# First weights, first blocks and first state of a recurrent loop brought into the stage before it: a two-branch kernel on one core

## The chip, the cores and the metric

One Trainium2 chip, one of its cores. The metric is device time in microseconds from start to end of one execution. Engines are named as in the profile: PE (TensorE matmul), PEld (its weight load), DVE (VectorE), ACT (ScalarE), POOL (GpSimd), SP (SyncE, which issues most DMAs; its queue is SPq). POOL issues DMAs too (POOLq). L339 is line 339 of the kernel before.

## The reference, cut to what matters

The output is two independent branches side by side. Branch A is a transformer layer with a memory of 8 rows that runs over 64 segments of 32 rows; each segment needs the memory that the one before it left. Branch B is a long convolution: a kernel K is summed from exponentials and applied to u by FFT.

```python
def A(x, mem0, Wq, Wk, Wv, Wo):            # x 2048x1024, 32 heads of 128
    mem = mem0                              # 8 x 1024
    for s in range(64):
        h = concat([mem, x[32*s:32*s+32]])
        q, k, v = h @ Wq, h @ Wk, h @ Wv    # each weight 1024 x 4096
        p = softmax(where(mask, q k^T * scale, -1e9))
        o = (p v) @ Wo                      # 4096 x 1024
        mem, outs[s] = o[:8], o[8:]

def B(u, A, B, C, log_dt, Dskip):           # u 2048 x 1024, state 128
    K = einsum(C, exp(dt*A*l), dt*B).real   # 1024 x 2048
    y = irfft(rfft(pad(u)) * rfft(pad(K)))[:2048] + u*Dskip
```

Everything is bfloat16 at the borders. The four weights of A are 33.6 MB together, in units of 128x2048 (512 KB); 64 units make up one segment.

## The kernel before

The program has three stages, one after the other, whose order of instructions on each engine is the order in which they are written (a manual schedule; the framework adds the semaphore waits).

**Tables** (up to about 490 us). `part_b` builds the Fourier matrices `MF` (ACT sines), transposes x, projects the rows of A that don't depend on the memory (`Ahead.projections`), transforms u into `Ud` in DRAM (`side`), and makes the tables of K over 16 blocks in an order written out by hand (`ORDER`). K goes to DRAM as `Kd`. In round f = 15 its first half (512 of 1024 columns) is read back as `KT` (L938 on SP), and POOL negates half of that into `KN` (`negate`, L974, at the word "u0" of `ORDER`).

**Transform** (about 488 to 746 us). 16 rounds b (L1238 on). Round b issues: the spectrum matmuls of b+1 (`spectrum`, L989, 64 matmuls reading `MF`, `KT` and `KN`), the copies `odd` on ACT, `pointwise` of b on DVE (ten 128x1024 operations, L1162 to L1173, reading `uq`, which SP loads two rounds ahead, L965), and from b = 4 on two inverse blocks (`inverse`, L1216, 64 matmuls reading the inverse matrices `MI` and their negated copies `mn`, then ACT `yb`, two DVE operations and a store by POOL, L1226). Eight more inverse blocks follow the last round; their inputs `Bt` are complete only when `pointwise` of round 15 is. Round b reads only column block kc = b mod 4 of `MF`, but `MF` is laid out by row block first. In round 0 POOL reads the second half of K (31 DMAs, L938) and SP loads three weight units; `negate` of the second half is on ACT in round 6 (L976), ahead of that round's inverse blocks.

**Weights that stay.** Of the 64 units, 45 stay in SBUF over all segments, 2 (`KEPT`: k,0,7 and o,15) stay in PSUM and are copied out piece by piece on DVE (`words`, `fetch`, L278), and 17 are streamed from DRAM in every segment through five slots `wst` (L256). 34 of the 45 are loaded by the generator `residents` during the transform: 3 in round 0, 4 in round 6, 8 in round 14, the rest between the last eight inverse blocks. They go into tiles that are dead by then: `kst`, `MF`, `xTl`, `wsl`, and a pool over the transform's work tiles. The other 11 are loaded where the first segment first uses them (`unit`).

**Loop** (`part_a`, about 746 us to the end). Before it, POOL makes the constants (identity, masks), PE transposes `mem0` into the state `hT`, SP loads the two KEPT units, and DVE puts them in PSUM. Each segment: k, q, v of both halves (L339), scores, softmax, output projection (L438), new state. The loop's weights come in the order of use; SP waits at each streamed unit until the slot's last reader on PE is done.

The KEPT units are loaded like this (L280 to L282), into the slots that the first streamed units also take:

```python
    for i, key in enumerate(KEPT):
        t_ = wst.tile([128, 2048], BF16, name="wst", tag="w%d" % i)
        nc.sync.dma_start(out=t_[:].rearrange("e (h d) -> e h d", h=2) if key[0] == "o" else t_[:], in_=src(key))
```

Of the kernel before, what the change touches and what calls it, by code (L numbers as in the profile page):

```python
# [29 lines left out]
SLOTS = 5  # L30
# [147 lines left out]

RESIDENT = [(m, t, kc) for t in range(2) for m in "kq" for kc in range(8)] + [("v", t, kc) for t in range(2) for kc in range(8)] + [("o", u) for u in range(16)]
RESIDENT = [key for key in RESIDENT if key not in streamed_keys() and key not in KEPT]  # L180


class Keys(list):
    pass


EARLY = (3, 13)


def load_resident(tc, pool, src, key, W_res, eng=None, t_=None):  # L190
    if t_ is None:
        t_ = pool.tile([128, 2048], BF16, name="W_%s" % "_".join(str(i) for i in key))
    (eng or tc.nc.sync).dma_start(out=t_[:].rearrange("e (h d) -> e h d", h=2) if key[0] == "o" else t_[:], in_=src(key))
    W_res[key] = t_


def part_a(ctx, tc, x, mem0, src, WD, HE, seg_len, out_a, ahead, W_res, rest):
    nc = tc.nc
    S, Dm = x.shape
    M = mem0.shape[0]  # L200
    SL = seg_len
    E = 128
    KC = Dm // 128
    NS = S // SL
    assert SL == 32 and M == 8 and Dm == 1024 and HE == 4096
    XM = 24
    XL = SL - XM
    NK = SL + M
    scale = float(E ** -0.5)

    const = ctx.enter_context(tc.tile_pool(name="a_const", bufs=1))
    XTd, PKd, OLd = ahead.XTd, ahead.PKd, ahead.OLd

    ctx.enter_context(tc.manual_schedule())
    ctx_w = rest.ctx
    wst = ctx_w.enter_context(tc.tile_pool(name="a_wst", bufs=1, side="right"))
    wres = ctx_w.enter_context(tc.tile_pool(name="a_wres", bufs=1, side="right"))
# [19 lines left out]
    nc.gpsimd.affine_select(out=BDL[:], in_=BDL[:], compare_op=ALU.is_ge, fill=0.0, base=7, pattern=[[8, 4], [32, 4]], channel_multiplier=-1)  # L237

    loads = [0]
# [4 lines left out]
    def unit(key):  # L244
        if key in rest:

            rest.remove(key)
            load_resident(tc, wres, src, key, W_res)
        if key in W_res:
            return W_res[key]  # L250
        if key in kept:
            return ahead_of.pop(key)
        between.pop(key, lambda: None)()
        t_ = wst.tile([128, 2048], BF16, name="wst", tag="w%d" % (loads[0] % SLOTS))
        loads[0] += 1
        nc.sync.dma_start(out=t_[:], in_=WD[key][:])  # L256
        return t_

    hT = const.tile([128, KC, SL], BF16, name="hT")
    with tc.tile_pool(name="a_m0", bufs=1) as pm0, tc.tile_pool(name="a_pm0", bufs=1, space=PSUM) as ppm:  # L260
        m0 = pm0.tile([M, Dm], BF16, name="m0")
        nc.scalar.dma_start(out=m0[:], in_=mem0)
        pm = ppm.tile([128, KC, M], BF16, name="pm")
        for kc in range(KC):
            nc.tensor.transpose(out=pm[:, kc, :], in_=m0[:, kc * 128:(kc + 1) * 128], identity=ident[0:M, 0:M])
        nc.vector.tensor_copy(out=hT[:, :, XM:SL], in_=pm[:])
# [13 lines left out]
    for i, key in enumerate(KEPT):  # L280
        t_ = wst.tile([128, 2048], BF16, name="wst", tag="w%d" % i)
        nc.sync.dma_start(out=t_[:].rearrange("e (h d) -> e h d", h=2) if key[0] == "o" else t_[:], in_=src(key))  # L282
        kept[key] = [ps_k.tile([128, 512], F32, name="keep", tag="keep%d" % (2 * i + n)) for n in range(2)]
        for n in range(2):
            words(kept[key][n][:], t_[:, 1024 * n:1024 * n + 1024])
# [31 lines left out]
    put_xt(load_xt(0))  # L317
# [9 lines left out]

    fetch(("k", 0, 7))
    for s in range(NS):
# [267 lines left out]
def part_b(ctx, tc, u, A_re, A_im, B_re, B_im, C_re, C_im, log_dt, Dskip, out_b, ahead, copies, residents):  # L597
# [22 lines left out]
    MF = ahead.pool.tile([128, 16, 2, 512], BF16, name="MF", tag="MF")  # L620
# [10 lines left out]
    with tc.tile_pool(name="b_par", bufs=1) as par, tc.tile_pool(name="b_parh", bufs=2) as parh, tc.tile_pool(name="b_mg", bufs=2) as mg, \  # L631
# [50 lines left out]

        def matrices():

            tms, kMs = {}, {}
            for c in range(0, 20, 2):
                if 4 <= c:
                    tm = tms.pop(c - 4)
                    v.tensor_scalar(out=tm[:].bitcast(I32), in0=tm[:].bitcast(I32), scalar1=0x7FFFFFFF, scalar2=None, op0=ALU.bitwise_and)
                    sc.activation(out=MF[:, c - 4:c - 2, 0, :], in_=tm[:], func=ACT.Sin, scale=-TWO_PI, bias=hp[:])  # L690
                if 2 <= c < 18:
                    tm = tms[c - 2]
                    v.scalar_tensor_tensor(out=tm[:], in0=kMs.pop(c - 2)[:], scalar=MAGIC, in1=tm[:], op0=ALU.subtract, op1=ALU.subtract)
                    sc.activation(out=MF[:, c - 2:c, 1, :], in_=tm[:], func=ACT.Sin, scale=-TWO_PI)
# [108 lines left out]

    kxp = ctx1.enter_context(tc.tile_pool(name="b_kx", bufs=2))
    tmp = ctx1.enter_context(tc.tile_pool(name="b_tmp", bufs=2))
# [18 lines left out]
    def matrices_back():  # L824
        for c in range(16):
            mt = take([128, 2, 4, 128], BF16, "mt")
            for kc in range(4):
                for cs in range(2):
                    pe.transpose(out=mt[:, cs, kc, :], in_=MF[:, c, cs, 128 * kc:128 * kc + 128], identity=ident[:])
# [7 lines left out]
    def side():  # L837

        uvs = [load_uq(0), load_uq(1)]
        for dq in range(4):  # L840
# [3 lines left out]
            for kc in range(4):  # L844
                got = {}
                for r in (0, 2, 1, 3):
                    ps = take([128, 2, DQ], F32, "ups")
                    for cs in range(2):
                        for mc in range(4):
                            pe.matmul(ps[:, cs, :], lhsT=MF[:, 4 * r + mc, cs, 128 * kc:128 * kc + 128], rhs=uv[:, 4 * r + mc],  # L850
# [79 lines left out]
    def load_k(dh, qs, KT):  # L930
        dsl = slice(DH * dh, DH * dh + DH)
# [39 lines left out]
    def negate(KT, eng=None):  # L971
# [3 lines left out]
        else:  # L975
            sc.activation(out=KN[:], in_=KT[:, 8:16, :], func=ACT.Copy, scale=-1.0)  # L976
        KNs.append(KN)

    def spectrum(b, s_):
        dq, kc = b // 4, b % 4  # L980
        KT, KN = ks[dq // 2], KNs[dq // 2]
        d = slice(DQ * (dq % 2), DQ * (dq % 2) + DQ)
        for half in range(2):
# [396 lines left out]
```

## Time and profile before

| what | value |
|---|---|
| time, median of 3 runs | 2421.98 us (2419.69 to 2426.86) |
| the profiled execution, its own time | 2430.37 us |
| its span | 2428.7 us |
| PE, DVE, ACT, POOL busy | 83%, 61%, 40%, 14% of the span |
| moved by DMA | 759.08 MB, mean 313 GB/s |
| last matmul of the transform | 741.2 us |
| first matmul of the loop | 754.9 us |
| end of segment 0 (first `ob`, L527, start) | 795.38 us |
| last `ob`, segment 63 | 2368.5 us, so 24.97 us for a segment |

How to read it: a row of a timeline gives start and duration in us, engine, line, operation, output and input, and in brackets how long the engine sat idle before it and what released it. A table of windows gives for each stretch its length, the busy time of each engine with the number of instructions, the granted TensorE clock, the busy share of the DMA engines, and GB/s. A table of waits gives for "who <- whom" the total, the number and the longest wait in us.

### The profile page before, as it was taken

What the parts mean: (1) busy time and instruction counts of PE and PEld (TensorE: products, weight loads), DVE (VectorE), ACT (ScalarE), POOL (GpSimd) and SP (SyncE); (2) the same over time, 40 slices, a digit from 0 to 9 for tenths busy, and PEclk for the clock granted to TensorE, in tenths of its full rate; (3) what the DMA queues carried; (4) which work ended last, traced back from release to release, by engine and by line L of the source; (5) the groups of instructions that cost most, each with busy time, mean ns of one, the idle gap of its engine ahead of it and who ended that gap; (6) DMA issues with size and microseconds to landing.
All of it is one profiled execution on the core that took longest, in us unless ns stands there. A gap on an engine that the chain in (4) does not pass through costs nothing.

```text
span 2428.7 us, 78387 instructions
## 1 busy us (share of the span) xinstructions
PE 2009.3 (83%) x33798; PEld 1184.6 (49%) x33798; DVE 1480.1 (61%) x3159; ACT 976.1 (40%) x1598; POOL 345.6 (14%) x578
## 2 busy tenths in 40 slices
PE   1699999669996888888888888888888888888879
PEld 1366665558883444444444444444444444444444
DVE  9599999989972445455554545454545545454540
ACT  6699999603332233232333333332323233332321
POOL 2235445541121000000000000000000000000020
PEclk6799999879997899999999999999999999999999
DMA  6686974583368999999999999999999999999992
GB/s 160 183 250 195 255 213 146 163 254 138 116 251 313 374 360 365 382 367 384 370 380 379 386 387 383 383 374 376 370 369 374 376 384 365 383 367 380 386 385 75
DMA packets 379376, 759.08 MB, mean 313 GB/s; under 512 B 121144, under 2 KB 213272, under 8 KB 376980
## 3 DMA queue, kind: packets, MB, share of 16 engines
q1 hardware_dynamic: 365236, 710.86, 81.3%
q0 software_dynamic: 13776, 43.19, 5.3%
q8 instruction: 264, 4.33, 0.7%
q14 instruction: 84, 0.69, 0.1%
q10 hardware_dynamic: 16, 0.02, 0.0%
HBM read 699.16 MB, written 67.88 MB: 316 GB/s over the span
## 4 chain that ended last, share of the span: by engine, by line
DMA 34%; PE 26%; DVE 9%; issue 6%; ACT 3%; SPq 1%; POOL 1%; ACTq 0%; DVEq 0%; POOLq 0%
DMA wst<-WD_k 15%; PE acc L339 13%; DMA wst<-WD_o 12%; PE pp L438 3%; DMA wst<-WD_v 2%; PE pe L561 2%; PE tr L350 2%; DMA out_dram<-uu 2%; DMA wst<-WD_q 2%; DVE piece L278 2%; ACT ev L345 1%; PE hps L989 1%; DMA W_o<-in_A_Wo_dram 1%; PE yp L1216 1%; DVE ob L527 1%
## 5 line engine op out<-in xcount | busy, mean ns | idle before, releaser
L339 PEld LDWEIGHTS <-hT 128*32 128x32 bf16 x12352 | 328.4, 97 | 472.0 <-issue 251.4
L339 PE MATMUL acc<-wst,hT 128*32 128x512 bf16 x3072 | 313.7, 392 | 166.5 <-DMA wst<-WD_k 74.5
L345 ACT CAST ev<-acc 128x512 bf16<-128x512 f32 x384 | 224.7, 585 | 411.9 <-PE acc L339 406.0
L339 PE MATMUL acc<-W,hT 128*32 128x512 bf16 x4608 | 366.2, 388 | 0.0
L438 PEld LDWEIGHTS <-oT 128*32 128x32 bf16 x8192 | 204.8, 97 | 120.5 <-issue 95.3
L278 DVE TENSOR_SCALAR piece<-keep 128x256 int32<-128x256 int32 (+1 forms) x640 | 191.6, 363 | 58.0 <-PE pp L438 31.3
L438 PE MATMUL pp<-W_o,oT 128*32 128x256 bf16 x5120 | 212.5, 276 | 7.3 <-DMA W_o<-in_A_Wo_dram 7.2
L377 DVE TENSOR_REDUCE mx<-sc 128x8 f32<-128x320 f32 x128 | 62.4, 487 | 247.3 <-PE sc L370 247.2
L339 PE MATMUL acc<-W_v,hT 128*32 128x512 bf16 x3072 | 210.9, 379 | 0.0
L351 DVE COPY KT<-tr 128x512 bf16<-128x512 bf16 x64 | 27.2, 425 | 262.6 <-PE tr L350 262.6
L438 PE MATMUL pp<-wst,oT 128*32 128x256 bf16 x2560 | 129.3, 279 | 41.8 <-DMA wst<-WD_o 32.9
L358 POOL COPY KT<-pk 128x128 bf16<-128x128 bf16 x128 | 37.6, 294 | 806.8 <-PE sc L370 448.7
L351 ACT COPY QT<-tr 128x512 bf16<-128x512 bf16 x128 | 74.9, 586 | 192.1 <-PE tr L350 191.2
L425 ACT CAST oT<-pv 128x512 bf16<-128x512 f32 x128 | 74.9, 585 | 168.7 <-PE pv L411 166.4
L312 POOL COPY hT<-xt 128x192 bf16<-128x192 bf16 x64 | 22.2, 347 | 736.7 <-DMA xt<-XTd 536.2
L989 PEld LDWEIGHTS <-MF 128*128 128x128 bf16 x1024 | 104.4, 102 | 44.3 <-issue 24.3
L158 PE MATMUL pro<-xTl,wsl 128*128 128x512 bf16 x512 | 120.1, 386 | 5.2 <-ACT xTl L102 5.2
L1216 PE MATMUL yp<-Bt,MI 128*128 128x256 bf16 x768 | 114.9, 276 | 3.6 <-DVE Bt L1173 3.6
L379 ACT ACTIVATE sc<-sc 128x320 f32<-128x320 f32 x128 | 54.0, 422 | 153.6 <-DVE sc L378 149.6
L989 PE MATMUL hps<-KT,MF 128*128 128x256 bf16 x720 | 95.7, 286 | 20.6 <-DVE x L1163 17.5
L350 PEld LDWEIGHTS <-ev 128*128 128x128 bf16 x1024 | 58.4, 98 | 98.2 <-issue 67.9
L350 PE MATMUL tr<-a_ident,ev 128*128 128x128 bf16 x1024 | 102.5, 223 | 1.0 <-ACT KT L351 1.0
(302 smaller groups left out, 3704.6 us busy)
## 6 DMA issues: line engine op xcount, KB each, us to landing
wst<-WD_o SPq DMA_DIRECT2D x320, 512.0 KB
wst<-WD_k SPq DMA_DIRECT2D x256, 512.0 KB
wst<-WD_q SPq DMA_DIRECT2D x256, 512.0 KB
wst<-WD_v SPq DMA_DIRECT2D x256, 512.0 KB
Ud<-ux POOLq DMA_DIRECT2D x16, 1024.0 KB, 5.6
uq<-Ud SPq DMA_DIRECT2D x32, 512.0 KB
pk<-PKd SPq DMA_DIRECT2D x64, 192.0 KB
wsl<-in_A_Wk_dram SPq DMA_DIRECT2D x16, 512.0 KB
```

The costliest lines, as they stand in the source:

```text
L158: nc.tensor.matmul(a[:], lhsT=w[:, kc, 128 * j:128 * j + 128], rhs=xTl[:, kc, :, :].rearrange("p s k -> p (s k)"), start=(kc == 0), stop=( ...
L278: nc.vector.tensor_scalar(out=out.bitcast(I32), in0=in_.bitcast(I32), scalar1=0, scalar2=None, op0=ALU.bitwise_or)
L339: nc.tensor.matmul(a[32 * g:32 * g + 32, o_:o_ + rhs.shape[1]], lhsT=hT[:, kc, :], rhs=rhs, start=(kc == 0), stop=(kc == KC - 1), tile_pos ...
L345: nc.scalar.copy(out=q[:], in_=a[:])
L350: nc.tensor.transpose(out=p[:, i, hl, :, :].rearrange("p a b -> p (a b)"), in_=q[:, 128 * hl:128 * hl + 128], identity=ident[:])
L351: eng(out=dst, in_=p[:, i, :, :, :])
L377: nc.vector.tensor_reduce(out=mx[:], in_=sc, axis=AX.X, op=ALU.max)
L379: nc.scalar.activation(out=sc, in_=sc, func=ACT.Exp, scale=scale)
L425: nc.scalar.copy(out=o[:], in_=p[:].rearrange("p a (g q) -> p a g q", g=4))
L438: nc.tensor.matmul(po[32 * qt:32 * qt + 32, :], lhsT=oT[:, h % 4, (h % 16) // 4, :], rhs=columns(w, 1024 * hh + 256 * qt, 256)[0][1], star ...
L989: pe.matmul(s_[r][half][:, cs, :], lhsT=MF[:, 4 * rr + mc, cs, 128 * kc:128 * kc + 128], rhs=rhs, start=(i == 0 and mc == 0), stop=(i == 1 ...
L1216: pe.matmul(yp[:, b, :], lhsT=m_[:, b, cs, kc, :], rhs=Bt[:, kc, j, half, c_, :], start=(n == 0), stop=(n == 15), skip_group_check=True)
```

## The change

- `MF` is laid out by column block first, so that a finished column block is 32 KB a partition in one piece.
- `KT` of the second half of K is two tiles of 256 columns instead of one of 512 (62 DMAs by POOL instead of 31, the same bytes). These, the `MI` matrices (eight tiles of 4 KB a partition instead of one) and the three first weight units move to one pool on the right side of SBUF. `mn` and the tiles of the inverse blocks get places of their own, and `odd` has one buffer instead of two.
- The weight loads are spread otherwise: one in each of rounds 1 to 3, four in round 6, two in 11 and 12, four in 13 and 14, then 10, 5 and one at a time in the last eight inverse blocks. They go over `kst`, the dead column blocks of `MF`, the two `KT` tiles, `xTl`, `wsl`, four new tiles, and dead `MI` tiles.
- The five slots `wst` are opened before the transform ends, and the first five units that the loop takes through them are loaded there. The unit o,15 is loaded in the loop, ahead of v,0,0 of segment 0.
- The loop's constants are made in round 4, `mem0` and the first x are loaded there, and the state is made in round 13 (8 transposes on PE, a copy on DVE, a copy on POOL).
- After round 15, three quarters (kc 0 to 2) of the matmuls of the first three of the last eight inverse blocks are issued before the blocks themselves.
- `negate` of the first half stands at the word "m'" of `ORDER` in round 15 instead of "u0"; that of the second half stands behind round 6's inverse blocks instead of before them, in two operations.

```diff
-EARLY = (3, 13)
+EARLY = (3, 4)
+LATE = 5
...
-    MF = ahead.pool.tile([128, 16, 2, 512], BF16, name="MF", tag="MF")
+    MF = ahead.pool.tile([128, 4, 16, 2, 128], BF16, name="MF", tag="MF")
...
-            if f == 15 and word == "u0":
+            if f == 15 and word == "m'":
                 negate(ks[0], gp)
...
+    pool = ahead.ctx.enter_context(tc.tile_pool(name="a_wre1", bufs=1, side="right"))
+    KT2 = [pool.tile([128, 16, DQ], BF16, name="KT", tag="KT%d" % i) for i in range(2)]
+    MI = [pool.tile([128, 2, 2, 4, 128], BF16, name="MI", tag="MI%d" % i) for i in range(8)]
...
+    def inverse_begin(dq, c, yp):
+        ready.append(negated(c)) if len(ready) * 2 <= c else None
+        early[dq, c] = yp
+        products_back(yp, dq, c, *ready[c // 2], range(3))
...
         if b == 0:
-            ks.append(load_k(1, (gp,), ktp.tile([128, 16, DH], BF16, name="KT", tag="KT")))
-            for _ in range(EARLY[0]):
-                next(resident)
+            ks += [load_k(DQ * i, DQ, (gp,), KT2[i - 2]) for i in (2, 3)]
...
-        if b == 6:
-            negate(ks[1])
-            for _ in range(4):
-                next(resident)
-        if b == 14:
-            for _ in range(8):
-                next(resident)
...
+        for _ in range({1: 1, 2: 1, 3: 1, 6: 4, 11: 2, 12: 2, 13: 4, 14: 4}.get(b, 0)):
+            next(resident)
+        if b == 4:
+            state = first_state(iv.tile([8, D], BF16, name="m0", bufs=1), iv.tile([128, 8, 24], BF16, name="xt0", bufs=1))
+            next(state)
+        if b == 13:
+            state.send(ps_y.tile([128, 8, 128], BF16, name="yp", tag="yp")[:, :, 0:8])
         if b >= 4:
             inverses(2)
+        if b == 6:
+            negate(ks[1:])
+    begun = [ps_h.tile([128, 2, 2, DQ], F32, name="hps", tag="h") for _ in range(2)]
+    for n_ in range(3):
+        inverse_begin(3, 2 * n_, begun[n_ // 2][:, n_ % 2])
     ctx2.close()
-    for _ in range(8):
+    for n_ in range(8):
         inverses(1)
-        for _ in range(3):
+        for _ in range((10, 5)[n_] if n_ < 2 else 1):
             next(resident, None)
-    for _ in resident:
-        pass
...
+        ahead.wst = ctx_w.enter_context(tc.tile_pool(name="a_wst", bufs=1, side="right"))
...
+        for i, key in enumerate((("k", 0, 7), ("k", 0, 0), ("k", 0, 5), ("q", 0, 1), ("q", 0, 5))):
+            first[key] = t_ = ahead.wst.tile([128, 2048], BF16, name="wst", tag="w%d" % i)
+            tc.nc.sync.dma_start(out=t_[:], in_=WD[key][:] if key in WD else src(key))
+            yield
...
+    def first_state(m0, xt):
+        nc = tc.nc
+        hT = constants(tc, const, ahead)
+        nc.sync.dma_start(out=xt[:].rearrange("p k r -> p (k r)"), in_=ahead.XTd[0])
+        nc.sync.dma_start(out=m0[:], in_=A_mem0[0])
+        pm = yield
+        for kc in range(8):
+            nc.tensor.transpose(out=pm[:, kc, :], in_=m0[:, kc * 128:(kc + 1) * 128], identity=ahead.consts[0][0:8, 0:8])
+        nc.vector.tensor_copy(out=hT[:, :, ahead.XM:], in_=pm)
+        nc.gpsimd.tensor_copy(out=hT[:, :, 0:ahead.XM], in_=xt[:])
+        yield
...
-    for i, key in enumerate(KEPT):
+    def load_kept(key):
...
+    load_kept(("k", 0, 7))
     fetch(("k", 0, 7))
+    between["v", 0, 0] = lambda: load_kept(("o", 15))
```

## The prediction

> **What bounds the kernel now.** I read the windows by stage first, then the timelines of SP and DVE at the two places where the stages change hands, then the waits.
>
> ```profile
> 600.00:640.00 40.00, 40.00 (x369) 35.84 (x367) 37.80 (x41) 11.49 (x24) 8.67 (x12) 1.00 0.32 107
> 680.00:720.00 40.00, 36.38 (x319) 31.81 (x317) 34.85 (x40) 14.14 (x26) 7.96 (x11) 0.96 0.75 268
> 720.00:760.00 40.00, 25.74 (x239) 20.64 (x238) 9.07 (x23) 11.38 (x20) 12.93 (x35) 0.80 0.74 272
> 760.00:800.00 40.00, 27.42 (x422) 12.50 (x425) 13.04 (x36) 8.49 (x16) 0.64 (x2) 0.71 1.03 395
> 1000.00:1500.00 500.00, 423.83 (x8608) 223.33 (x8609) 261.33 (x726) 155.68 (x302) 19.00 (x61) 0.99 1.00 380
> ```
>
> After the stretch come PE, PEld, DVE, ACT, POOL, then clock, DMA share, GB/s. The transform (600 to 640) keeps PE busy all the time with DVE at 94% and DMA at a third; the loop (from 760) keeps DMA at 1.00 with PE at 85%. So transform time is PE time, loop time is bytes, and a byte moved from the loop into the transform costs nothing there. Between the two neither is full:
>
> ```profile
> 496.27 9.59 SPq L124 DMA_DIRECT2D PKd<-PVd  x8
> 505.90 1.48 SPq L1141 DMA_DIRECT2D Dsk<-in_B_Dskip_dram  x1
> 508.19 1.42 SPq L193 DMA_DIRECT2D W_k<-in_A_Wk_dram  x3
> 509.70 1.58 SPq L965 DMA_DIRECT2D uq<-Ud  x2
> ...
> 714.78 12.00 SPq L193 DMA_DIRECT2D W_v<-in_A_Wv_dram  x11
> 746.27 0.33 SPq L282 DMA_DIRECT2D wst<-in_A_Wk_dram  x1
> ```
>
> ```profile
> 735.00:742.00 7.00, 6.18 (x57) 5.28 (x54) 1.53 (x5) 2.14 (x5) 3.42 (x16) 1.00 0.55 205
> 742.00:749.00 7.00, 0.34 (x8) 0.27 (x8) 0.52 (x2) 0.00 (x0) 2.38 (x10) 0.66 0.29 78
> 749.00:756.00 7.00, 1.08 (x12) 0.53 (x16) 3.89 (x9) 0.00 (x0) 0.34 (x1) 0.50 0.69 240
> ```
>
> SP issues no load from 726.8 to 746.3: the next tile lies over the inverse blocks' tiles and waits for the last store (four waits of SP on `out_dram<-uu`, 19.2 us). PE ends the transform at 741.2 and starts the loop at 754.9. Segment 0 then ends at 795.38 (`ob`), 54.2 us after the last matmul of the transform. Three stalls stand inside the transform:
>
> ```profile
> 522.28 1.23 DVE L1167 TENSOR_TENSOR y<-uq,x 128x1024 f32<-128x1024 f32 x1 [7.62 <-DMA uq<-Ud]
> ```
>
> ```profile
> PE yp L1216 <- DVE Bt L1173: 3.6, 1, 3.6
> PE yp L1216 <- ACT mn L1188: 2.9, 1, 2.9
> ```
>
> **The change, part by part**, as what it takes from the end of segment 0. From there on the same 17 units, stores and instructions follow in the same order with the same waits, 24.97 us a segment, and the same final projection, so the gain passes through unchanged.
>
> *Three weight loads out of round 0.* DVE is ready for `uq` of round 2 at 514.66 (513.45 + 1.21), and it lands at 522.2. From 500 to 536 the DMA share is 1.0. On SP's queue ahead of `uq` stand eight PKd copies, Dsk and three weight units; the units (1.57 MB) go to rounds 1 to 3, behind `uq`. At the 357 GB/s of 512 to 522 they took 4.4 us, and SP issues `uq` up to 2.3 us earlier (509.70 against the end of Dsk, 507.38). I put the landing at 516.3, so 1.6 us of the stall stay and **6.0 us** go. Ends: 0 (the queue is full anyway, and K's second half now comes in 512-byte rows) and 7.6. The chain of waits goes from DVE here into PE at 534, so PE gets what DVE gets.
>
> *K in 62 pieces instead of 31.* POOL issued 31 in 498.5 to 520.4, 0.71 us each; 62 end at about 545, at the 0.55 us of those without a wait at 536. Behind them on POOL stand the five `uu` loads of the first inverse blocks, then the constants. The first `uu` is used at 557.1 (551 after the gain), and one takes 2.7 us to land: cover of 3 us at the slow pace. Cost 0; without the cover, 1 to 4 us. K itself is first used in round 7, at 585.
>
> *`negate` of the first half.* The Trainium skill, page "SBUF — State Buffer", section "Who interferes with whom", says that VectorE in a two-port mode and GpSimd contend for one pair of ports, and the second to issue blocks until the first is done. The row:
>
> ```profile
> 460.40 10.57 POOL L974 TENSOR_SCALAR KN<-KT 128x4096 bf16<-128x4096 bf16 x1 [1.27 <-DMA PVd<-vst]
> 462.51 9.44 DVE L1050 TENSOR_SCALAR nr<-nr 128x1856 int32<-128x1856 int32 x1
> ```
>
> The same operation took 1.6 us a round before (441.79), so the block costs 7.8 us. By the rule alone, an earlier place in the order would free them. But the bracket says that a DMA released it, not POOL: the last of the 31 KT loads was issued by SP up to 458.4, two microseconds before 460.4. Those don't move. The only POOL instruction passed is one store of `MId` (0.56 us), not needed until round 3. I take 0; the ends are 0 and 7.8 (the latter would need K earlier).
>
> *`negate` of the second half behind round 6's inverse blocks.* ACT ran it for 3.64 us at 579.96, ahead of `mn`, and PE waited 2.9. Now it starts when the second block's `yb` are out (about one us after PE goes on to the spectrum), and its first piece, 1.8 us, is needed 4.1 us into that spectrum (36 matmuls that read only KT). **2.9 us**; ends 0 and 2.9.
>
> *State and constants.* The constants took 4 us on an idle POOL (739.9 to 743.9); in round 4 they run beside `pointwise`, where DVE has 0.8 us a round to spare and can be a few us late without holding PE. 0; at worst 3. The 8 transposes in round 13 take one of two PSUM buffers, and by the waits in the built program the round's second block then waits for the copy (0.66 us) of the first: **-0.9 us**.
>
> *Three inverse blocks begun.* PE idled 3.62 us for `Bt`, and then eight blocks took 28.5 us (712.71 to 741.2) at a clock of 0.79 at first, where 3.49 us a block make 27.9. Now 3 x 3/4 x 3.49 = 7.9 us of them fill the gap. Gained 3.6 + 0.6, lost 0.9 since the second block shares a PSUM tile with the first and waits for its `yb`: **3.3 us**; ends 0 and 4.2.
>
> PE so ends the transform 6.0 + 2.9 - 0.9 + 3.3 = 11.3 us earlier, at 729.9.
>
> *Units placed over dead tiles.* The 27 units that were issued from 693.8 on become 12 in rounds 11 to 14, where two thirds of DMA are free, and 20 after (five of them the loop's first). Fourteen of these wait until `pointwise` of round 15 is done (about 705); with 2 MB of `uu` they are 9.3 MB, 24 us at 385 GB/s: in by 730, as PE ends. On SP they stand behind the `uq` of rounds 13 to 15, which are needed 11 us after issue while two units take 2.8. In MI's eight loads of 512 KB for four of 1 MB a rule speaks against the change: the skill's "DMA: Bandwidth & Descriptors", section "Measured (HBM→SBUF, 128 partitions, SWDGE, issued from GpSimd)", wants 1 MB or more for 75% of peak; by its fixed 2.0 us (section "Anatomy of one DMA"), one after another, four more loads would add 8 us. The row of the loop, 512 KB a load at 380 GB/s with up to eight in flight, makes it nothing. I take the row.
>
> *The handover.* Before: 54.2 us from PE's last transform matmul to `ob`. After: k,0,7 and k,0,0 lie in their slots and the state is ready. SP's first blocked load (k,1,0) waits for DVE to empty slot 0: `yb` 0.7 and the last two `uu` operations 0.5 after PE's end, then two copies of 0.63, 2.5 us together. From there 12 streamed units, o,15 and 11 resident ones, 24 x 0.524 MB and 0.25 MB of pk and xt, at 380 GB/s: 33.8 us; the last one lands and is used 2.4 us later (in the loop the last pp takes 1 us and `ob` follows 0.3 after). Sum 38.7, **15.5 us** less. PE needs about 24 us for a segment, so it stays under that. Ends: 9 (the 1.6 us a unit that segment 0 needs before, 48 us for 30, on 24 units, and 7 us of start) and 27 (no idle DMA at all from 705 on).
>
> Sum 11.3 + 15.5 = 26.8. Against its own execution: 2430.37 - 26.8 = 2403.6; against the median, which is 8.4 us lower, 2421.98 - 26.8 = **2395.2 us**.
>
> **Rivals.** *The front stays full* (20%): 512-byte rows and MI use the room that the units leave, `uq` still lands at 521 to 522, or `uu` comes late by what is gained. For it: DMA at 1.0 until 536. Against: bytes ahead of `uq` on its own queue fall by a third. 2395 + 6 = 2401. *The handover packs better* (13%): the loads fill DMA so that segment 0 ends with its transfers from 694 on, 44 units at 1.38 us and 4 us of `uu`, near 760. For it: 399 GB/s in 699 to 738. Against: eight in flight, and five slots that only the loop frees. Gain 35 to 40, so 2384. *Longer segments* (4%): slots and resident tiles lie elsewhere, the segment is DMA bound at 1.00, and every wait added there counts 63 times. It decides from 26.8/63 = 0.43 us a segment; at 0.6 the time is 2395 + 38 = 2433. For it: only that no slack exists. Against: the waits listed for the loop's loads are those of before. *It doesn't do what it says* (5%): the loads in rounds 11 to 14, waiting on SP for the last spectrum matmul of their column block, hold the `uq` behind them, and each round stretches. Four rounds at 2 us, gain 19, 2403. Against: that spectrum ends before the `pointwise` which frees the `uq` tile.
>
> **How the numbers follow.** 58% for 2395, with its own range 2388 to 2402 from the ends of `uq` and the handover. Of the rivals, the first and the last lie at 2401 to 2404, the second at 2384: with those two sides in, 2381 to 2406 holds 8 in 10. 0.3% is 7 us, about what a measurement of this kernel can tell from no change. Slower by more: 4%, the third rival. Within: 3%, where several gains fail together. Faster: 93%.
>
> **What would show it.** Right: no SP gap between the last resident load and a slot load; DVE's stall before L1167 of round 2 under 3 us; no `yp` wait on `mn` in round 6; PE going from the last `yp` to `acc` within 2 us at a clock of 1.00; segment 0 over 35 to 42 us after that; 24.9 to 25.0 us a segment. Wrong: a DVE stall on `uu` at round 4, `uq` waits in rounds 12 to 15, KN starting well before 460, or segments longer than 25.3 us.

## The result, and the profile after

The changed kernel takes 2396.86 us (median of 4 runs, 2393.12 to 2401.22) where the kernel before takes 2423.1 us (median of 4): a ratio of 0.9892, with a 95% interval of 0.9865 to 0.9919. That is 26.2 us less; the forecast was 26.8. The profiled execution takes 2401.22 us against 2430.37 us, 29.2 us less.

Windows of the changed kernel, with the columns as before (length, PE, PEld, DVE, ACT, POOL, clock, DMA share, GB/s):

```profile
600.00:640.00 40.00, 40.00 (x369) 35.85 (x367) 38.57 (x43) 13.81 (x26) 8.67 (x12) 1.00 0.37 117
...
680.00:720.00 40.00, 38.76 (x354) 34.35 (x353) 29.90 (x38) 16.86 (x29) 9.41 (x13) 1.00 0.81 287
720.00:735.00 15.00, 13.90 (x152) 10.48 (x150) 5.47 (x14) 3.85 (x10) 6.07 (x9) 1.00 1.00 368
735.00:742.00 7.00, 5.54 (x109) 2.37 (x105) 1.42 (x3) 3.25 (x5) 0.30 (x1) 1.00 1.03 406
742.00:749.00 7.00, 5.71 (x111) 2.51 (x112) 6.40 (x17) 3.18 (x7) 0.00 (x0) 1.00 0.96 346
749.00:756.00 7.00, 2.66 (x45) 1.28 (x44) 2.81 (x7) 0.59 (x1) 0.00 (x0) 0.85 1.03 378
...
1000.00:1500.00 500.00, 419.60 (x8564) 220.01 (x8557) 259.91 (x721) 155.45 (x302) 18.87 (x61) 0.99 1.00 375
```

The transform is still PE's and the loop still the DMA engines'. What is gone is the hole between them: from 742 to 749 PE was busy for 0.34 us of 7 at a DMA share of 0.29, and is now busy for 5.71 us at 0.96. PE goes from the last inverse matmul (it ends at 729.06) to the first `acc` of the loop (728.99) without a pause.

SP's timeline at the two places where the stages change hands:

```profile
506.80 1.47 SPq L1161 DMA_DIRECT2D Dsk<-in_B_Dskip_dram  x1
508.39 1.29 SPq L981 DMA_DIRECT2D uq<-Ud  x2
...
707.52 0.53 SPq L1384 DMA_DIRECT2D wst<-in_A_Wk_dram  x1
...
711.09 7.80 SPq L223 DMA_DIRECT2D W<-in_A_Wv_dram  x5
728.97 0.33 SPq L312 DMA_DIRECT2D pk<-PKd  x1
731.44 0.82 SPq L268 DMA_DIRECT2D wst<-WD_k  x2
...
759.82 0.38 SPq L223 DMA_DIRECT2D W_o<-in_A_Wo_dram  x1
```

`uq` of round 2 (508.39) now has only `Dsk` and the PKd copies ahead of it, and the first slots are loaded at 707.5. The gap from 718.9 to 729.0 is still in SP's queue, but not in the DMA engines, which work off what was issued (share 1.00 from 720 to 735). So "no gap in SP's queue" was the wrong sign to look for; the DMA share was the right one.

On DVE, the operation that waited 7.62 us for `uq`, and on PE the waits of inverse blocks:

```profile
516.70 1.23 DVE L1187 TENSOR_TENSOR y<-uq,x 128x1024 f32<-128x1024 f32 x1 [1.03 <-DMA uq<-Ud]
```

```profile
PE yp L1240 <- ACT yb L1256: 0.8, 1, 0.8
PE hps L1240 <- ACT yb L1256: 0.7, 1, 0.7
...
PE yp L1240 <- ACT mn L1208: 0.5, 1, 0.5
```

The wait for `uq` is 1.03 us here (the other profiles with the weight units behind `uq` show none), and the 2.9 us for `mn` and the 3.6 us for the last `Bt` are gone. Of PE's waits the first line is round 13 with its state transposes, the other two are the begun blocks.

Where the 29.2 us of the profiled executions are, by places that both traces have:

| stretch | before | changed | gained |
|---|---|---|---|
| up to PE's first matmul of round 1's spectrum | 487.69 | 488.90 | -1.2 |
| from there to PE's last inverse matmul | 253.5 | 240.2 | 13.3 |
| from there to the first `ob` (end of segment 0) | 54.2 | 41.3 | 12.9 |
| from there to the last `ob` (63 segments) | 1573.2 (24.97 each) | 1567.7 (24.88 each) | 5.5 |
| the rest of the profiled time | 61.8 | 63.2 | -1.3 |

### The profile page after: what moved, and what is told of

It reads as the page before. It is cut to its first block, busy times and chain, and to the rows that moved or that the text cites. A ratio compares the mean times of both kernels' runs of the same rounds, so it can differ in the third digit from the quotient of the medians.

```text
span 2399.5 us, 78400 instructions
## 1 busy us (share of the span) xinstructions
PE 1998.7 (83%) x33773; PEld 1177.4 (49%) x33798; DVE 1481.3 (62%) x3159; ACT 976.9 (41%) x1599; POOL 360.1 (15%) x609
## 4 chain that ended last, share of the span: by engine, by line
PE 38%; DMA 30%; DVE 20%; ACT 7%; issue 4%; SPq 1%; DVEq 0%; ACTq 0%; POOL 0%; POOLq 0%
DMA wst<-WD_k 16%; PE acc L349 12%; DMA wst<-WD_o 8%; PE yp L1240 4%; PE hps L1007 4%; PE pp L448 3%; DVE nr L1068 2%; PE pe L571 2%; DMA wst<-WD_q 2%; PE pro L158 2%; DMA wst<-WD_v 2%; PE tr L360 2%; PE ups L866 2%; PE pa L1037 2%; DVE piece L282 1%
## 5 line engine op out<-in xcount | busy, mean ns | idle before, releaser
L349 PE MATMUL acc<-W,hT 128*32 128x512 bf16 x5120 | 399.7, 383 | 0.2 <-DMA W<-in_A_Wv_dram 0.2
L448 PE MATMUL pp<-W_o,oT 128*32 128x256 bf16 x4096 | 182.5, 276 | 6.1 <-DMA W_o<-in_A_Wo_dram 6.1
L349 PE MATMUL acc<-MF,hT 128*32 128x512 bf16 x2048 | 159.5, 385 | 0.0
L1240 PE MATMUL yp<-Bt,MI 128*128 128x256 bf16 x680 | 102.8, 273 | 0.8 <-ACT yb L1256 0.8
```

The lines of the kernel that those rows point to most:

```text
L349: nc.tensor.matmul(a[32 * g:32 * g + 32, o_:o_ + rhs.shape[1]], lhsT=hT[:, kc, :], rhs=rhs, start=(kc == 0), stop=(kc == KC - 1), tile_pos ...
L448: nc.tensor.matmul(po[32 * qt:32 * qt + 32, :], lhsT=oT[:, h % 4, (h % 16) // 4, :], rhs=columns(w, 1024 * hh + 256 * qt, 256)[0][1], star ...
L1240: pe.matmul(yp[:, b, :], lhsT=m_[:, b, cs, kc, :], rhs=Bt[:, kc, j, half, c_, :], start=(kc == 0 and cs == 0 and half == 0), stop=(kc == 3 ...
```

## The experiments

Every experiment is an edit of the changed kernel; "ACT, three tiles" starts from the version with the first negate on ACT. This table has the places of their profiles, one profile for each row; each section reads its own row. The handover is the stretch from PE's last inverse matmul to the first `ob`, the fourth column. The ratios are to the kernel before, measured beside each version (medians of 2423.1 to 2427.6 us). Runs of one kernel differ by 24 us and more (the changed kernel: 2383 to 2408), and much of it can come from the loop, whose order of instructions none of these edits changes after segment 0: the mean segment lies between 24.74 and 24.97 us from profile to profile, without relation to the edit. So steps of 1 to 6 us are read from the profile's places, and the times are only held against them. Where an edit doesn't touch a stretch, the column "to PE's end" repeats within 1 us (239.3 to 240.2), "to first `ob`" within 2, and the start of round 1 lies between 487.2 and 489.7.

| run | round 1 starts | to PE's end | to first `ob` | first `ob` | time, median | ratio to before (95%) |
|---|---|---|---|---|---|---|
| before | 487.7 | 253.5 | 54.2 | 795.4 | 2423.1 | |
| changed | 488.9 | 240.2 | 41.3 | 770.4 | 2396.9 | 0.9865 to 0.9919 |
| changed, again | 488.3 | 239.8 | 42.2 | 770.3 | 2393.5 | 0.9837 to 0.9901 |
| weights back in round 0 | 488.2 | 243.6 | 41.6 | 773.3 | 2402.4 | 0.9889 to 0.9947 |
| none begun | 489.7 | 245.2 | 41.2 | 776.0 | 2401.5 | 0.9882 to 0.9933 |
| loads after round 15 | 489.7 | 240.1 | 42.5 | 772.3 | 2402.7 | 0.9875 to 0.9940 |
| negate on ACT | 477.9 | 239.4 | 41.1 | 758.4 | 2384.9 | 0.9805 to 0.9884 |
| negate on ACT, again | 476.8 | 239.5 | 41.3 | 757.6 | 2389.7 | 0.9822 to 0.9875 |
| loads behind the uq tiles | 487.2 | 239.3 | 60.7 | 787.1 | 2415.4 | 0.9950 to 0.9981 |
| slots behind | 488.5 | 239.5 | 50.8 | 778.8 | 2412.5 | 0.9920 to 0.9967 |
| ACT, three tiles | 477.7 | 238.9 | 44.1 | 760.7 | 2392.5 | 0.9823 to 0.9896 |
| weights back, K late | 487.7 | 243.4 | 42.2 | 773.3 | 2403.3 | 0.9866 to 0.9941 |
| K in 31 loads | 488.3 | 239.7 | 43.0 | 771.0 | 2401.8 | 0.9874 to 0.9939 |
| negate before round 6's blocks | 489.2 | 243.1 | 42.3 | 774.6 | 2405.2 | 0.9874 to 0.9935 |

### The three weight units back in round 0

```diff
         if b == 0:
             ks += [load_k(DQ * i, DQ, (gp,), KT2[i - 2]) for i in (2, 3)]
+            for _ in range(3):
+                next(resident)
...
-        for _ in range({1: 1, 2: 1, 3: 1, 6: 4, 11: 2, 12: 2, 13: 4, 14: 4}.get(b, 0)):
+        for _ in range({6: 4, 11: 2, 12: 2, 13: 4, 14: 4}.get(b, 0)):
```

> The changed kernel with one part undone: the three weight units of rounds 1 to 3 are issued in round 0 again, on SP ahead of uq of round 2. My theory (their bytes stood before uq on a full DMA): uq of round 2 lands 5 to 6 us later, DVE waits 6 to 8 us there instead of 1.0, PE ends the transform at 734 to 735 instead of 729.0, and the kernel takes 5 to 6 us more than the changed one. Rival (the front is full whatever stands in it, and uq came earlier for another reason, such as MI in smaller pieces): the DVE wait stays at 1 to 2 us and PE's end within 1 us of 729.

DVE's timeline of this run:

```profile
519.50 1.23 DVE L1187 TENSOR_TENSOR y<-uq,x 128x1024 f32<-128x1024 f32 x1 [4.58 <-DMA uq<-Ud]
```

The wait comes back, but only in part: 4.6 us, and PE's transform is 3.4 to 3.8 us longer than in the two profiles of the changed kernel. Weight units ahead of `uq` on SP's queue are a cause, of 3.4 to 3.8 us and not of the 5 to 6 expected.

### K's second half out of the way, and K in 31 loads

Against the start of round 1, `uq` let PE go on 46.7 us later before (534.36 - 487.69), 43.4 us later with the weights back, 39.9 and 38.7 us in the two profiles of the changed kernel. So 3.2 us come from something else. Two runs were to ask whether K's loads are it.

```diff
         if b == 0:
-            ks += [load_k(DQ * i, DQ, (gp,), KT2[i - 2]) for i in (2, 3)]
+            for _ in range(3):
+                next(resident)
+        if b == 1:
+            ks += [load_k(DQ * i, DQ, (gp,), KT2[i - 2]) for i in (2, 3)]
```

> The run with three weight units back in round 0, and in addition the 62 loads of K's second half issued one round later. It asks where the other 3 us went by which uq of round 2 came earlier (7.6 us of waiting became 1.0, the weight units alone gave back only 3.6). Theory (K's loads share the full DMA with uq, and they start 6 us later on POOL in the changed kernel): with K out of the way DVE's wait for uq of round 2 falls from 4.6 to under 2.5 us. Rival (K's loads do not touch uq; MI or the clock did it): it stays within 1 us of 4.6. In both, uu of the first inverse blocks comes later, and PE may wait in rounds 4 to 8.

POOL's timeline with the weights back (first line) and in this run (second), then DVE's wait in this run:

```profile
502.65 8.16 POOL L954 DMA_DIRECT2D KT<-Kd  x15 [3.70 <-DMA PKd<-PVd]
502.53 8.22 POOL L954 DMA_DIRECT2D KT<-Kd  x15 [4.00 <-DMA PKd<-PVd]
```

```profile
DVE y L1187 <- DMA uq<-Ud: 3.9, 1, 3.9
```

The edit did not hold K's loads back. They stand a round later in the program, but POOL has nothing else to wait for between the two places and starts them at 502.5 us all the same. So this run is a repeat of the one before, and 4.6 against 3.9 us of waiting (243.6 against 243.4 us to PE's end) is scatter; it says nothing about K. The next expectation, which counts 0.7 us for it, was built on this misreading. The second run loads K as before, and two of its weight units move from round 13 to round 14:

```diff
-    KT2 = [pool.tile([128, 16, DQ], BF16, name="KT", tag="KT%d" % i) for i in range(2)]
+    KT2 = pool.tile([128, 16, DH], BF16, name="KT", tag="KT2")
...
-            ks += [load_k(DQ * i, DQ, (gp,), KT2[i - 2]) for i in (2, 3)]
+            ks += [load_k(DH, DH, (gp,), KT2)]
```

> The changed kernel with K's second half in one tile and 31 loads of 1 KB rows, as before the change, instead of 62 of 512-byte rows; POOL starts them at the same time. Of the 6.8 us by which uq of round 2 lands earlier against the start of round 1, the three weight units explain 3.5; holding K's 62 loads back gave only 0.7. Theory (31 larger loads, eight in flight, take twice the bytes per us from the full DMA, so splitting them is what freed the rest): DVE's wait for uq of round 2 is 3 to 5 us instead of 1.0, and uu of the first inverse block no longer waits (2.2 us in the changed kernel). Rival (splitting has no part in it): the wait stays under 1.6 us; then the rest stays open.

DVE does not wait for `uq` at all, as the rival has it. But it doesn't in the second profile of the changed kernel either, so a delay of `uq` by larger loads is hidden here as long as it stays within DVE's slack, and the run does not decide. POOL's timeline of this run:

```profile
525.32 1.44 POOL L1200 DMA_DIRECT2D uu<-in_B_u_dram  x2
```

The inverse inputs `uu` are issued at 525.3 instead of 548.4, their wait of 2.2 us on DVE in round 4 is gone, and PE's transform is still 239.7 us: the wait that 62 loads put on DVE costs PE nothing.

Where the 3.2 us come from stays **open**, but the traces point at K. This is what DMAs issued by POOL moved from the start of round 1 until `uq` was there, in the kernel before (487.69 to 522.24) and with the weights back (488.15 to 519.45): packets, MB, share.

```profile
q0 software_dynamic: 1381, 2.00, 20.2%
q0 software_dynamic: 1056, 0.73, 10.4%
```

POOL's large loads there are those of K. Before, all 31 were issued by then; with the weights back they start 4.2 us later (502.65 against 498.48, since their tiles now wait for the PKd copies), and only 25 of 62 half-sized ones had been issued. At the 361 GB/s of 517.7 to 522.2 the 1.27 MB that are missing make 3.5 us, an estimate. The start and the size of K's loads would both do it, and no run changed either with the weights in front.

### None of the inverse blocks begun

```diff
-    begun = [ps_h.tile([128, 2, 2, DQ], F32, name="hps", tag="h") for _ in range(2)]
-    for n_ in range(3):
-        inverse_begin(3, 2 * n_, begun[n_ // 2][:, n_ % 2])
```

> The changed kernel without the three inverse blocks that are begun before the last Bt. My theory: PE waits 3.6 us for the last Bt again and runs the eight blocks whole, so it ends the transform 3.3 (as predicted) to 4.5 us (as the changed kernel's trace lets one read) later, and since the first slot load of the loop follows PE's end, segment 0 ends as much later. Rival (the DMA engines, full from 705 us on, set the end of segment 0): PE's end moves by 3 to 4.5 us and the end of segment 0 by less than 1.5 us.

Windows of this run (columns as above):

```profile
701.00:705.00 4.00, 0.49 (x5) 0.29 (x3) 3.93 (x4) 0.00 (x0) 0.19 (x1) 0.92 0.77 258
705.00:708.00 3.00, 2.83 (x14) 1.97 (x14) 2.79 (x7) 0.00 (x0) 0.58 (x1) 0.50 0.21 78
708.00:711.00 3.00, 3.00 (x16) 2.07 (x15) 1.00 (x3) 1.37 (x3) 1.60 (x3) 0.50 0.93 307
711.00:714.00 3.00, 3.00 (x29) 2.64 (x28) 0.08 (x1) 0.28 (x2) 0.00 (x0) 0.97 1.03 377
```

PE stands 3.7 us and then works at a granted clock of 0.50 for 6 us, with 14 and 16 matmuls in windows that hold 29 at full clock. The transform is 5.0 to 5.4 us longer, more than the top of the expected 3.3 to 4.5. The clock accounts for that: it is 0.50 from 704.33 to 711.16, 6.83 us, where in the kernel before, after a pause of 3.62 us, it is 0.50 for 3.41 us only (713.54 to 716.95). PE ran for 6.0 us of the first and all of the second, and the 2.6 us more at half clock cost 1.3: 5.0 instead of the 3.7 that the begun blocks gained against the kernel before. The Trainium skill's page "TensorE: Matmul & The Clock Gate", section "Part 1: The HAM clock gate", puts the fall at one idle window of about 3.4 us and the way back at one busy window of the same length. The stretches here are one and two such windows; the first of the two began 0.8 us before PE went on, so it was not busy throughout. The pauses of 0.5 to 1.1 us in the changed kernel left the clock at 1.00. And the handover is as long as in the changed kernel, 41.2 us: the end of segment 0 follows PE's end, as my theory has it: it comes 5.6 us later, where the rival has under 1.5.

### Twelve units after round 15, twice

```diff
-        for _ in range({1: 1, 2: 1, 3: 1, 6: 4, 11: 2, 12: 2, 13: 4, 14: 4}.get(b, 0)):
+        for _ in range({1: 1, 2: 1, 3: 1, 6: 4}.get(b, 0)):
...
-        for _ in range((10, 5)[n_] if n_ < 2 else 1):
+        for _ in range((22, 5)[n_] if n_ < 2 else 1):
```

> The changed kernel with the twelve weight units of rounds 11 to 14 issued only after round 15, together with those that follow there. My theory (the handover is bound by bytes from 705 us on): 12 x 0.524 MB at 385 GB/s are 16.3 us, so PE's end stays at 729 (within 1 us), and from there to the first ob it takes 55 to 58 us instead of 41.4; the kernel takes 12 to 17 us more. Rival (the handover gained because state and first blocks lie ready, not by the bytes moved): the end of segment 0 moves by under 4 us.

SP's timeline of this run:

```profile
641.94 30.83 SPq L981 DMA_DIRECT2D uq<-Ud  x6
672.82 2.32 SPq L223 DMA_DIRECT2D MF<-in_A_Wq_dram  x4
...
687.05 4.24 SPq L223 DMA_DIRECT2D W<-in_A_Wq_dram  x6
```

This run did not put the question it was made for. The units are later in the program, but SP issues them from 672.8 us on: nothing stands before them in SP's queue that waits for round 15. The handover is at most 1.2 us longer, and the time, 5.9 us above the changed kernel's, lies within the scatter. A load's place in the program says little; what the queue ahead of it waits for says when it starts. The next run puts the same twelve units behind the four that take over the `uq` tiles:

```diff
+        for _ in range(4):
+            put(ahead.pool.tile([128, 2048], BF16, name="W1", tag="wsl", bufs=4))
+            yield
...
+        for _ in range(EARLY[1]):
+            load_resident(tc, pool, src, rest.pop(0), W_res)
+            yield
         for n in range(2):
             for t_ in early[0:6] if n == 0 else early[6:8]:
...
-        for _ in range(4):
-            put(ahead.pool.tile([128, 2048], BF16, name="W1", tag="wsl", bufs=4))
-            yield
...
-        for _ in range(EARLY[1]):
-            load_resident(tc, pool, src, rest.pop(0), W_res)
```

> In the run before this one the twelve units left their rounds but not their time: SP issued them from 672.8 us on, since nothing that it waits for stood ahead of them. Here they stand behind the four units over the uq tiles, which wait for pointwise of round 15 (about 705 us). My theory (from 705 us on segment 0 is bound by bytes): 12 x 0.524 MB at 385 GB/s are 16.3 us, PE's end stays where it was and the first ob comes 12 to 17 us later than in the changed kernel, the kernel takes as much more. Rival (units loaded early buy next to nothing, as the small effect of the run before could also be read): the first ob moves by less than 4 us.

SP's timeline of this run, and then the waits of PE from 700 to 790 us:

```profile
703.05 1.76 SPq L223 DMA_DIRECT2D W_k<-in_A_Wk_dram  x4
704.91 1.12 SPq L223 DMA_DIRECT2D MF<-in_A_Wk_dram  x2
...
725.16 0.33 SPq L1384 DMA_DIRECT2D wst<-in_A_Wk_dram  x1
```

```profile
PE acc L349 <- DMA wst<-WD_k: 19.0, 2, 12.1
```

The four units over the `uq` tiles (`W_k`) are issued at 703 us, and now the twelve follow from 704.9 us on. The first slot load comes at 725 instead of 707.5, PE stands 12.1 us before the loop, and the first `ob` comes 16.7 us later, as expected. PE's end is 1.7 to 2.6 us earlier in this profile, so the handover takes 60.7 us, 18.5 to 19.4 more: 12 units at 1.4 us (16.3 us) and a little more. The time is 18.5 us above that of the changed kernel. From bytes that are moved out of the stretch behind 705 us the handover does gain.

### The slots over the inverse blocks' tiles

```diff
-        ahead.wst = ctx_w.enter_context(tc.tile_pool(name="a_wst", bufs=1, side="right"))
...
-        for i, key in enumerate((("k", 0, 7), ("k", 0, 0), ("k", 0, 5), ("q", 0, 1), ("q", 0, 5))):
-            first[key] = t_ = ahead.wst.tile([128, 2048], BF16, name="wst", tag="w%d" % i)
-            tc.nc.sync.dma_start(out=t_[:], in_=WD[key][:] if key in WD else src(key))
-            yield
...
     wres = ctx_w.enter_context(tc.tile_pool(name="a_wres", bufs=1, side="right"))
+    wst = ctx_w.enter_context(tc.tile_pool(name="a_wst", bufs=1, side="right"))
...
-    loads = [5]
+    loads = [0]
```

> The changed kernel with the loop's five slots over the inverse blocks' tiles, as before the change: no block of the loop is loaded ahead, the first waits for the last store of the inverse blocks; the weight units that lay there lie over the tiles of pointwise instead. My theory (what the handover gained at its start comes from slots that are free early): SP issues the first slot load 3 to 5 us after PE's end, PE stands 6 to 10 us with DMA part idle, and the first ob comes 5 to 11 us later than in the changed kernel. Rival (only the total of bytes counts, the order of the loads does not): under 3 us.

SP's timeline and the windows of this run:

```profile
707.27 10.58 SPq L223 DMA_DIRECT2D W<-in_A_Wv_dram  x5
731.85 0.33 SPq L291 DMA_DIRECT2D wst<-in_A_Wk_dram  x1
```

```profile
720.00:730.00 10.00, 8.03 (x74) 6.96 (x71) 2.03 (x5) 2.92 (x7) 4.20 (x7) 1.00 0.34 114
730.00:740.00 10.00, 2.73 (x28) 1.28 (x32) 2.67 (x7) 0.00 (x0) 0.20 (x1) 0.64 0.72 267
```

The hole of the kernel before is back: SP issues the first slot load 3.8 us after PE's end (728.0), the DMA engines are at 0.34 and 0.72 for 20 us, PE stands 9.2 us, and the handover takes 50.8 us, 8.6 to 9.5 more. The time is 16 us above that of the changed kernel, more than the profile's place shows; with runs from 2401 to 2429 us I don't read more from it.

### The second negate ahead of round 6's blocks

```diff
+        if b == 6:
+            negate(ks[1:])
         if b >= 4:
             inverses(2)
-        if b == 6:
-            negate(ks[1:])
```

> The changed kernel with the negation of K's second half back ahead of round 6's inverse blocks on ACT. My theory: PE waits 2.5 to 3.2 us for mn in round 6 and ends the transform as much later; segment 0 ends as much later too. Rival (PE has slack behind round 6, as DVE runs without a pause from 554 to 622 us): PE waits, but its end moves by less than 1 us.

Waits of PE from 500 to 740 us in this run:

```profile
PE yp L1240 <- ACT mn L1208: 3.6, 2, 3.1
```

3.1 us of it in round 6, the other 0.5 is there in the changed kernel too. PE's end comes 2.9 to 3.3 us later against the start of round 1. PE has no slack there although DVE runs without a pause.

### The first negate on ACT

```diff
-            if f == 15 and word == "m'":
-                negate(ks[0], gp)
             if f == 16 and word == ORDER[0]:
+                negate([ks[0][:, :, DQ * i:DQ * i + DQ] for i in range(2)])
```

> The changed kernel with the first half of K negated on ACT after its last sine instead of on POOL. My theory (in the trace VectorE's instructions beside the 10.57 us of POOL's KN, 9.84 and 5.66 us, are blocked by POOL and are not slow for another reason): the first of them takes 1.1 to 1.2 us unless POOL's ux adds now stand there, the spectrum of round 0 waits under 4 us for KN instead of 6.7, round 1 of the transform starts 6 to 10 us earlier (at 479 to 483 us instead of 488.9), and PE ends the transform 4 to 10 us earlier. Rival (the wait only moves on to uq of round 2, on a full DMA): round 1 starts earlier by as much, but DVE then waits 6 to 10 us more for uq, and PE's end moves by less than 2 us. Second rival (the durations have nothing to do with POOL): they stay near 10 and 5 us.

DVE and POOL of the changed kernel, from 460 us:

```profile
462.36 9.84 DVE L1068 TENSOR_SCALAR nr<-nr 128x1856 int32<-128x1856 int32 x1
472.12 5.66 DVE L1075 TENSOR_SCALAR wn<-sn 128x768 bf16<-128x768 bf16 x1
477.70 1.11 DVE L1068 TENSOR_SCALAR nr<-nr 128x1856 int32<-128x1856 int32 x1
```

```profile
460.65 10.57 POOL L990 TENSOR_SCALAR KN<-KT 128x4096 bf16<-128x4096 bf16 x1 [15.72 <-DMA PVd<-vst]
...
474.80 2.75 POOL L885 TENSOR_TENSOR ux<-us 128x256 f32<-128x256 f32 x4
```

The same operations on DVE, and the negation on ACT, in this run:

```profile
462.04 1.58 DVE L1068 TENSOR_SCALAR nr<-nr 128x1856 int32<-128x1856 int32 x1
463.54 0.88 DVE L1075 TENSOR_SCALAR wn<-sn 128x768 bf16<-128x768 bf16 x1
464.35 1.65 DVE L1068 TENSOR_SCALAR nr<-nr 128x1856 int32<-128x1856 int32 x1
```

```profile
463.56 3.69 ACT L993 ACTIVATE KN<-KT 128x2048 bf16<-128x2048 bf16 x2
```

POOL's 10.57 us are 3.69 us on ACT, which stood idle for 8.3 us there, and DVE's three operations take 1.58, 0.88 and 1.65 us instead of 9.84, 5.66 and 1.11. The second of them was held too, until POOL's last `ux` operations ended at 477.6, which the negation had pushed there. Round 1 starts 11.0 us earlier, nothing of it is lost at `uq`, and the first `ob` comes 12.0 us earlier. This fits the rule that the prediction quoted from the Trainium skill's page "SBUF — State Buffer", section "Who interferes with whom", and set aside for this change because the negation did not move: DVE's first operation ended 1.0 us after the negation did, its second 0.2 us after the last `ux`. No trace shows the ports themselves; the durations follow POOL, which rules out the second rival. And what it was worth here was not 7.8 us but 11, without K coming earlier.

> The first negate on ACT, against the changed kernel in the same call. My theory: the 11 to 12 us that the trace shows at the start of round 1 and at the end of segment 0 are there in the time too: 10 to 13 us less than the changed kernel. Rival (part of the earlier difference of 12 us is scatter of the loop between runs): 5 us or less.

In the profile the 12 us are there again (first `ob` at 757.6 against 770.3). In the times they are not: 2389.7 us against 2393.5 us is less than the rival's 5 us, after 2384.9 against 2396.9 us the first time. All ten runs of the changed kernel together have a mean of 2395.8 us and the eight of this version 2387.9 us. The version's ratio to the kernel before is 0.9822 to 0.9875 in the second measurement, and it is the best that was run; by how much it beats the changed kernel, these runs don't settle, since the loop behind it scatters by as much.

> The changed kernel again, as the measure for the other runs on this chip. Expected: 2390 to 2402 us; PE's end of the transform within 1.5 us of 729.0, the first ob within 2 us of 770.4, segments of 24.75 to 24.95 us on the mean.

The places repeat as expected, the second time within 0.1 us at the first `ob`; one run took 2383 and one 2408 us.

### Three tiles for the begun blocks

```diff
-    begun = [ps_h.tile([128, 2, 2, DQ], F32, name="hps", tag="h") for _ in range(2)]
+    begun = [ps_h.tile([128, 2, 2, DQ], F32, name="hps", tag="h") for _ in range(3)]
     for n_ in range(3):
-        inverse_begin(3, 2 * n_, begun[n_ // 2][:, n_ % 2])
+        inverse_begin(3, 2 * n_, begun[n_][:, 0])
```

> The version with the first negate on ACT, and each of the three begun inverse blocks in a PSUM tile of its own. My theory: the 0.75 us in which PE waited for yb of the first block go, nothing else moves: PE ends 0.7 us earlier than in the version with negate on ACT alone, the time is 2380 to 2390 us. Rival: the third tile waits for pointwise of round 15, and PE waits 1 us or more there: no gain or a small loss.

Waits of PE from 690 to 740 us in this run:

```profile
PE acc L349 <- DVE piece L282: 2.8, 1, 2.8
```

PE's wait for `yb` is gone and PE ends about 0.6 us earlier than with the first negate on ACT alone, but it then waits 2.8 us instead of 1.1 for the pieces of k,0,7, which DVE copies after its last `uu` operation, and that waited for its input from DRAM. The time, 2392.5 us, lies above the 2380 to 2390 expected. A miss that neither theory had: past PE's end the next thing late was a load. Whether three tiles made it late or this one profile did, no run shows.

## Why the prediction was right, step by step

The mechanism held in both places: the transform lost its stalls, and the handover its hole. At the first `ob`, where the parts end, the gain is 25.0 us of the 26.8. That the median came within 0.6 us is luck: runs of one kernel differ by 24 us, and in the profiled executions 5.5 us of loop scatter fill up what the handover lacks. Inside the sum, some terms were wrong in size, and two errors nearly cancel.

- **Three weight units out of round 0, 6.0 us.** Mechanism right, size wrong. The stretch gained 6.8 us (46.7 to 39.9), but the units carry 3.4 to 3.8 of it. The step that failed is "they took 4.4 us, and SP issues `uq` up to 2.3 us earlier", which puts the whole 6.0 us on the units. SP did issue `uq` 2.5 us earlier against the start of round 1 (19.5 instead of 22.0 us), but the units' return cost only 3.4 to 3.8.
- **K in 62 pieces, 0 us.** The other 3 us came from something that the sum had at nothing. The traces point at K: less of it was moved ahead of `uq`. The forecast had seen only the opposite, that its 512-byte rows fill the room. That it is K is argued, not shown; that it made up for the units is luck. The cover for `uu` was too thin, too: POOL reached `uu` at 548.4, and DVE waited 2.2 us; PE was not held by it, as K in 31 loads shows.
- **First negate at another word, 0 us.** Right within the scatter: round 1 starts 1.2 us later in the changed kernel's profile and 0.6 in its second, while profiles with the same front lie from 487.2 to 489.7. The end of 7.8 us that was kept for a freed port was too small: it counted L1050 alone and not what was held behind it. And it did not need K earlier: another engine was enough.
- **Second negate behind round 6, 2.9 us.** Right (2.9 to 3.3 when undone).
- **State and constants, -0.9 us.** Right: PE waits 0.8 us in round 13. It was not undone by itself.
- **Begun blocks, 3.3 us.** From the last matmul before the eight blocks' work PE took 33.4 us before (1.3 us of matmuls that don't need the last `Bt`, a wait of 3.62, then 28.46 us) and 29.7 us after (699.37 to 729.06): 3.7 us. Undone, it costs 5.0 to 5.4: the clock stayed at 0.50 for 6.83 us, twice as long as in the kernel before.
- **PE's end** was forecast 11.3 us earlier and comes 12.1 us earlier.
- **Units over dead tiles, 0 us beside the transform.** Right: PE's transform is as long with them as without (239.3 us). But the rounds in which they stand matter little; that their tiles are free before 705 us matters. No engine waits for `MI` in the changed kernel, so its eight smaller loads cost nothing, as taken.
- **The handover, 54.2 to 38.7 us.** It is 41.3, so 12.9 us instead of 15.5. The start was right: the first slot load is issued 2.4 us after PE's end (2.5 forecast). The term that failed is the stream, 33.8 us and 1.1 to land; it took 37.8 us, from 731.44 to 769.24. The chain of waits of the changed kernel, in order of time (start, length, what), and two stretches of the stream:

```profile
749.12 10.68 DMA W_o<-in_A_Wo_dram
759.82 9.38 DMA W_o<-in_A_Wo_dram
769.24 1.12 PE pp L448 x15
```

```profile
731.44:733.00 1.56, 1.21 (x9) 0.53 (x13) 1.35 (x5) 0.00 (x0) 0.00 (x0) 1.00 0.81 251
745.50:748.00 2.50, 2.31 (x66) 1.16 (x63) 2.44 (x7) 0.74 (x2) 0.00 (x0) 1.00 0.85 259
```

The count was wrong by one. Segment 0 needed 30 units before, and five are now loaded ahead, so 25 are left and not 24: SP issues 13 streamed units, o,15 and 11 resident ones from 731.44 to 759.82. That is 1.4 us of the 2.9. The other 1.5 us are not settled by a run. In the trace the engines are not full in the two stretches above, behind gaps in SP's queue, and at most 0.7 MB of segment 1's loads (1.8 us at 380 GB/s) were moved in the same time; elsewhere the rate is a little above 380. The 9.4 us that the last unit takes from its issue to its use are for the most part those of the loads ahead of it: with eight in flight (SP's ninth load waits until the first has landed), 8 x 0.524 MB at the 391 GB/s of 748 to 769 are 10.7 us, an estimate.

- **Segments unchanged.** 24.88 us against 24.97; the 5.5 us that this makes in the profiled executions lie within the scatter of the other profiles.

Of the rivals, a full front is out (1.03 us of waiting), better packing is out (41.3 us, not 30; the 399 GB/s in 699 to 738 that spoke for it are 383 in the trace), and loads that hold `uq` in rounds 12 to 15 are out: no such wait is there. Segments did not grow.

## What to carry to other kernels

Before a load is moved in the program, look at what the queue ahead of it waits for: twelve loads moved behind the last round started before it all the same, and only behind a tile that frees late did they cost their 19 us; K's loads, moved a round later, did not start later at all. Read the start in the trace before the result of such an edit. A hand-over from a compute-bound stage to a transfer-bound one is priced by the bytes that are left to move when the first ends, plus what the first load must wait for. And where an operation is slow beside a GpSimd instruction, price not that operation alone but everything that both engines push back behind it.

## What the runs showed that was not expected

A GpSimd negation of 10.57 us held VectorE through two operations, of which the second was held by other GpSimd operations that the first had delayed: 11 us in all, from one instruction that ACT does in 3.69 us. A pause of 3.7 us of PE was followed by 6 us at a granted clock of 0.50, so that it cost 5 us in all; after one of 3.62 us in the kernel before, only 3.41 us were at 0.50. And the same loop took 24.74 to 24.97 us a segment from one profile to the next, 14 us over the loop, which is half of what this change gained.
